# Sliding-window attention into a gated feed-forward block on one core: batch 2's first scores moved into the gate blocks of group 1, and two weight loads cut in half

## The chip, the cores and the metric

The kernel runs on one core of a Trainium2 chip. Its engines are TensorE (PE in the profile; PEld is its loading of weights), VectorE (DVE), ScalarE (ACT), GpSimd (POOL) and SyncE (SP), each with an instruction stream of its own that runs in order. 16 DMA engines, shared by all that issue transfers, move data. The metric is the device time of one execution in microseconds (us); the kernel before takes 339.22 us, the median of three runs (338.67 to 339.76).

## The reference

Two parts follow each other. The first is attention over 8 batches of 8 heads, 576 positions and 64 values a head. Each query sees itself and the 127 keys before it, with a penalty that grows with the distance at a slope of its own for each head:

```python
scores = scale * np.matmul(q, k.transpose(0, 1, 3, 2))
bias = slopes[:, None, None] * (-np.abs(rel).astype(np.float32))[None, :, :]
mask = (rel >= 0) & (rel < window)                      # window = 128
scores = np.where(mask, scores + bias[None], -1000000000.0)
attn = np.exp(scores - np.max(scores, axis=-1, keepdims=True))
attn = attn / (np.sum(attn, axis=-1, keepdims=True) + 1e-09)
out = np.matmul(attn, v)
```

The second takes the 8 x 576 = 4608 rows of 512 values that come out (the heads side by side), and puts them through a gated feed-forward block: `gelu(x @ w_gate) * (x @ w_val) @ w_out`, with 1536 columns between.

## The kernel before, in words

**Feed-forward.** The 4608 tokens are worked through in nine groups of 512. For each group, twelve gate blocks (`gate_val`, L623) of 128 columns each: four matmuls of 512 tokens with `w_gate`, four with `w_val`, each half into a PSUM bank of its own; ScalarE applies gelu to the first (L647) and VectorE multiplies it with the second (L648) into `hT`. Then sixteen out units (`out_part`, L670): three matmuls each of 128 tokens with `w_out` (L677), four units to a tile of 128 tokens in one PSUM bank, which VectorE or ScalarE copies out (L682) and SyncE stores (L667). Group 0 is special: its blocks are worked in pieces of 192, 384 and 128 tokens, as attention of batch 0 hands them over, and its weights come while it runs.

**Attention.** Attention lies between the parts of the groups: batch 1 in group 0, batch 2 and the scores of batch 3 in group 1, and in each later group the products of one batch and the scores of the next. Its steps are: queries and keys loaded by GpSimd (L112) and transposed by a DMA that SyncE issues (`transposes_dma`, L173); `scores` (L235) in two visits `s` of two pairs of heads each, with matmuls of 64x64 tiles (L216), exponentials on ScalarE (L229) and a multiplication by the decay mask on VectorE (L232); `values_and_sums` (L512), the products with v and with ones (L501) in two halves, whose sums are inverted by ScalarE as exp(-ln) (L531, L533) or by a reciprocal on VectorE (L529), and a scaling into the transposed input `xT` of the feed-forward (L537). `scores2` (L267) is a form for the batches from 3 on. ScalarE needs one function table for exponentials and one for gelu, and loads it when the function changes; `exp_table` (L938) loads the first ahead of need.

**Order.** The order in each engine's stream is written out by hand: it is the order of the calls. What lies between a group's gate blocks and the end of its out units is a list in `todo` (L921): a number is that many out units, `("s", b, s, pairs)` scores, `("pv+", b, half)` products, `("scale",)` the scaling that the products left over. PSUM has eight banks, and each tile of `bank()` (L68) takes one until its last reader is done.

**Loads.** GpSimd issues loads one after the other, and each waits until the eighth before it has landed. In places it first copies two values into `mark` (L949, L971, L987), which has it wait for what it copies: at L987, for the last of batch 2's transposed queries, before it issues the loads of batch 3's queries and keys and batch 2's v (L988, L989). At the start it loads batch 0's v, the weights of blocks 0 and 1 by themselves, v's last two blocks of rows, and the weights of blocks 2 and 3 together (L742 to L747).

**Batch 0's rest.** Tokens 384 to 575 of batch 0 are divided by their sums late: `products_rest` (L597) has ScalarE copy the products into `recip` and part of the sums (the last 64 tokens) into `inverse`, a float view of the tile `T`; `inverse_rest` (L609) takes reciprocals of the other 128 tokens straight from PSUM into `inverse`, and `inverse_next` (L613) those of the copied ones, in place; `scale_rest` (L617) multiplies.

**Halves.** `HALVED` (L29) names gate blocks whose matmuls are cut into two of 256 tokens, in both halves of the weights.

Of the kernel before, what the change touches and what calls it, by code (L numbers as in the profile page):

```python
# [26 lines left out]
HANDOVER = 720  # L27

HALVED = ((1, 0), (1, 1))  # L29


@with_exitstack
def kernel(
# [10 lines left out]
    nc = tc.nc  # L44
    B, H, S, D = q.shape
# [22 lines left out]
    def bank():  # L68
        return psum.tile([128, 512], FP32, name="ps")
# [7 lines left out]
    wg = consts.tile([128, 4, DFF], BF16, name="wg")  # L77
# [30 lines left out]
    def load(t, src, b, js=range(5), last=0):  # L108
        for j in js:
            n = rows(j)  # L110
            at = last if j == 4 else 0
            nc.gpsimd.dma_start(  # L112
                out=t[at:at + n, j, :].rearrange("p (h d) -> p h d", h=H),
                in_=src[b][:, 128 * j:128 * j + n, :].rearrange("h p d -> p h d"))
# [5 lines left out]
    def load_v(b, js=range(5)):  # L120
        load(vb[b % 2], v, b, js, 64)
# [20 lines left out]
    def load_w(lo, hi):  # L142
        for dst, src in ((wg, moe_w_gate), (wv, moe_w_val)):
            nc.gpsimd.dma_start(  # L144
                out=dst[:, :, lo:hi],
                in_=src[:, lo:hi].rearrange("(c p) f -> p c f", p=128))
# [44 lines left out]
    def prob(b):  # L191
        return Ps[b % 2].rearrange("p (c i) n -> p c i n", i=2)
# [21 lines left out]
    def score(b, c, i, m, q0, n, out, first=True):  # L214
        half = slice(64 * i, 64 * i + 64)
        nc.tensor.matmul(  # L216
            out=out, lhsT=keys(b, c, m)[half, :], rhs=qT[b % 2][half, c, q0:q0 + n],
            start=first, stop=True, skip_group_check=not first)

    def blocks(n, x):  # L220
        if n == 3 and x:
            return ((7, 448, 128, 0), (8, 512, 64, 128))
        return ((2 * n + x, 128 * n + 64 * x, 192, 0),)
# [11 lines left out]
    def scores(b, s, cs, later=None):  # L235
        pss = []
        for c in cs:
            ps = [bank(), bank()]
            pss.append(ps)
            for n in (2 * s, 2 * s + 1):  # L240
                for x in (0, 1):
                    for m, q0, w, skip in blocks(n, x):
                        for i in (0, 1):
                            col = 192 * (n - 2 * s) + skip
                            score(b, c, i, m, q0, w, ps[i][64 * x:64 * x + 64, col:col + w])
        for c, ps in zip(cs, pss):
            dst = prob(b)[:, c, :, 64 + 384 * s:448 + 384 * s]
            for i in (0, 1):
                exp(dst[:, i, :], ps[i][:, 0:384])
            args = (dst, decay(s, c))  # L250
            if later is None:
                mask(*args)
            else:
                later.append(args)
# [142 lines left out]
    sumrow, recip = {}, {}  # L397
# [188 lines left out]
    def scale_first(c, x, ps):  # L586
# [6 lines left out]
    lo0 = PARTS[0][1][0]  # L593
    inverse = T.rearrange("p h x -> p (h x)").bitcast(FP32)[:, 0:4 * (S - lo0)].rearrange(
        "p (c x) -> p c x", c=4)

    def products_rest():  # L597
        w = S - lo0
        pss = products(0, [(2 * n, slice(2 * n, 2 * n + 2), lo0, S, 0) for n in (0, 1)] + [
            (1 + c // 2 * 2, c, lo0, S, w * (c % 2)) for c in range(4)])  # L600
        for n in (0, 1):
            nc.scalar.copy(out=recip[0][:, 2 * n:2 * n + 2, lo0:S],
                           in_=pss[1 + 2 * n][:, 0:2 * w].rearrange("p (c x) -> p c x", c=2))
        for n in (0, 1):
            nc.scalar.copy(out=inverse[:, 2 * n:2 * n + 2, 128:w],
                           in_=pss[2 * n][:, 0:2 * w].rearrange("p (c x) -> p c x", c=2)[:, :, 128:w])
        return pss

# [2 lines left out]
        nc.vector.reciprocal(inverse[:, c, 0:128], pss[c // 2 * 2][:, at:at + 128])  # L611

    def inverse_next(n):  # L613
        to = inverse[:, 2 * n:2 * n + 2, 128:S - lo0]
        nc.vector.reciprocal(to, to)

    def scale_rest(lo, hi):  # L617
        nc.vector.tensor_tensor(out=xT[:, :, lo:hi], in0=recip[0][:, :, lo:hi],
# [4 lines left out]
    def gate_val(g, f, lo=0, hi=512, later=None):  # L623
        if g not in hid:
            hid[g] = h_pool.tile([128, NF, 512], BF16, name="hT")
        t0 = 512 * g % RING
        n = hi - lo

        if n > 256 or lo >= 384:
            pg, pv = bank()[:, 0:n], bank()[:, 0:n]  # L630
            order = [(w, ps, c, c == 0) for w, ps in ((wg, pg), (wv, pv)) for c in range(4)]
        else:
            ps = bank()
            pg, pv = ps[:, 0:n], ps[:, n:2 * n]
            order = [(w, ps, c, w is wg and c == 0)
                     for cs in ((0, 1), (2, 3)) for w, ps in ((wg, pg), (wv, pv)) for c in cs]
        cols = ((0, 256), (256, 512)) if (g, f) in HALVED else ((0, n),)
        for w, ps, c, begins in order:
            for a, e in cols:
                nc.tensor.matmul(  # L640
                    out=ps[:, a:e], lhsT=w[:, c, 128 * f:128 * (f + 1)], rhs=xT[:, c, t0 + lo + a:t0 + lo + e],
                    start=begins and a == 0, stop=(c == 3),
                    skip_group_check=n <= 256 and lo < 384 or len(cols) > 1)

        def act():
            gl = g_pool.tile([128, 512], BF16, name="gelu")
            nc.scalar.activation(out=gl[:, 0:n], in_=pg, func=AF.Gelu)  # L647
            nc.vector.tensor_tensor(out=hid[g][:, f, lo:hi], in0=pv, in1=gl[:, 0:n],  # L648
                                    op=ALU.mult)

        if later is None:
            act()
        else:
            later.append(act)
# [77 lines left out]
    for h in (0, 2, 4, 6):  # L732
        for w, src in ((0, q), (1, k)):
            (nc.scalar if w and h == 0 else nc.sync).dma_start(
                out=raw[w][h // 4].rearrange("p (h x) -> p h x", h=4)[:, h % 4:h % 4 + 2, :],
# [7 lines left out]
    load_v(0, (0, 1, 2))  # L743
    load_w(0, 128)
    load_w(128, 256)
    load_v(0, (3, 4))
    load_w(256, 512)  # L747

    for h in range(H):
        nc.vector.memset(slope1[:, h:h + 1], -8.0 * 2.0 ** (-8.0 * (h + 1) / H))  # L750
# [6 lines left out]
    for x in (0, 1):  # L757
        half, to = slice(64 * x, 64 * x + 64), slice(64 * x, 64 * x + 192)
# [104 lines left out]
    masks, waiting = [], []  # L863
# [42 lines left out]
    for n in range(4):  # L906
        nc.gpsimd.dma_start(
            out=wo[:, 3 * n:3 * n + 3, :],
# [5 lines left out]
    for t in (qs[0], ks[0]):  # L914
# [5 lines left out]
    scales = []  # L920
    todo = {  # L921
        0: [("table",), ("s", 1, 0, (0, 1)), ("o", 0, 0, 0), ("o", 0, 1, 0), ("s", 1, 0, (2, 3)), ("o", 0, 0, 1), ("s", 1, 1, (0, 1)), ("o", 0, 1, 1), ("s", 1, 1, (2, 3), masks), ("pv+", 1, 0), 4, ("transposes", 2), ("pv+", 1, 1), 4],
        1: [("table",), ("s", 2, 0, (0, 1)), 3, ("s", 2, 0, (2, 3)), 2, ("s", 2, 1, (0, 1)), 2, ("s", 2, 1, (2, 3), masks), ("pv+", 2, 0, scales), 1, ("scale",), 2, ("pv+", 2, 1), 1, 2, ("s2", 3, 0), ("add", 3, 0), 3, ("s2", 3, 2), ("add", 3, 2, None, (0,))],
    }

    def steps(g):
# [11 lines left out]
    def exp_table():  # L938
        nc.scalar.preload_act_table_set("natural_log_exp_and_others")
# [4 lines left out]
    for g in range(NG):  # L944
        if 1 <= g < B - 2:
            transposes_dma(3 if g == 1 else g + 2)
        if g == 1:

            nc.gpsimd.tensor_copy(out=mark, in_=kT[1][0:1, 0, 512:514])  # L949
            load_qk(4)  # L950
            load_v(3)
        for f in range(9 if g == 0 else 0, NF):
            gate_val(g, f)
            if g == 2 and f == 2:
                add(3, 2, act, (1,))
            if g == 0 and f == 10:
                masks_of_last_blocks(0, 8)
            if g == 0 and f == 9:
                for c in range(4):
                    for w in (0, 1):  # L960
                        transpose(1, w, c, (act, dve)[w])
            if 2 <= g < B - 1:
                if f == (4 if g == 2 else 3):
                    sums4(g + 1)
                if f == (6 if g == 2 else 5):
                    gather(g + 1)
                if f == (8 if g == 2 else 7):
                    spread_dma(g + 1)
                if f == 9 and g + 2 < B:

                    nc.gpsimd.tensor_copy(out=mark, in_=hid[g][0:1, f, 0:2])  # L971
                    if g + 3 < B:
                        load_qk(g + 3)
                    load_v(g + 2)
        if g == 0:
            nc.gpsimd.memset(Ps[0][:, :, 0:64], 0.0)
            for t in (qs[1], ks[1]):
                nc.gpsimd.memset(t[64:128, 4, :], 0.0)
        for item in steps(g):
            if isinstance(item, int):  # L980
                out_part(g, item)
            else:
                RUN[item[0]](*item[1:])
        store()
        if g == 0:

            nc.gpsimd.tensor_copy(out=mark, in_=qT[0][0:1, 0, 512:514])  # L987
            load_qk(3)  # L988
            load_v(2)  # L989
# [30 lines left out]
```

## Time and profile before

| what | value |
| --- | --- |
| median of 3 runs | 339.22 us (338.67, 339.76) |
| the profiled execution's own time | 338.56 us |
| its span, first to last instruction | 336.8 us |
| TensorE busy | 331.0 us, 98% of the span |
| VectorE, ScalarE, GpSimd busy | 191.9, 170.7, 108.2 us |
| granted TensorE clock | 1.000 |
| chain that ended last | TensorE 83%, DMA 11%, GpSimd 4% |
| GpSimd's DMA queue | 107456 packets, 18.10 MB |

The profile is of one execution. Busy is the share of time in which an engine has an instruction under way; for TensorE, whose matmuls overlap, 98% says that it seldom stops, not that it runs at its peak. The chain goes back from the last instruction, at each step to what released it. In a timeline a row has start, length, engine, line, instruction, what is written and read and how often, and in brackets the idle time before it and what ended that. In the chain of waits a row has start, length and what; "issue" is time in which the engine waited for nothing that the profile shows. For a load, start is its issue on GpSimd; it has landed when all sixteen DMA engines have reported.

### The profile page before, as it was taken

The numbers are of one execution on the slowest core, as the hardware profiler recorded it, in microseconds if no ns is written. First come the engines' busy times: TensorE is split into PE (matmuls) and PEld (weight loads), VectorE is DVE, ScalarE is ACT, GpSimd is POOL, SyncE is SP. The second block draws the span as 40 slices with busy tenths as digits, with TensorE's granted clock in tenths as the row PEclk, the third lists the DMA queues.
The fourth block names the chain that finished last, engine by engine and source line by source line (L and its number), as shares of the span: only waits on it lengthen the run. The fifth ranks groups of instructions, "written<-read, shape, count | busy, mean of one in ns | idle before, by whom it ended". The sixth has DMA issues, their size and how long they took to land.

```text
span 336.8 us, 8136 instructions
## 1 busy us (share of the span) xinstructions
PE 331.0 (98%) x3316; PEld 169.3 (50%) x3316; DVE 191.9 (57%) x359; ACT 170.7 (51%) x320; POOL 108.2 (32%) x144
## 2 busy tenths in 40 slices
PE   8999999999999999999999999999999999999996
PEld 5657656544554454445544554445444544444444
DVE  7768876435779557945694469536964324303320
ACT  7974687437796339332943375335732133223322
POOL 6974784293094193009500870050000000000000
DMA  8999999999999899969985999495106110020002
GB/s 208 170 198 189 203 166 177 132 167 143 192 148 161 197 168 210 157 144 131 191 168 91 161 179 183 78 173 90 65 2 140 64 65 0 1 95 31 0 31 95
DMA packets 149914, 43.49 MB, mean 129 GB/s; under 512 B 133588, under 2 KB 142836, under 8 KB 149876
## 3 DMA queue, kind: packets, MB, share of 16 engines
q0 software_dynamic: 107456, 18.10, 70.9%
q1 hardware_dynamic: 39104, 18.62, 24.0%
q10 hardware_dynamic: 3316, 6.25, 8.1%
q8 instruction: 26, 0.43, 0.5%
q14 instruction: 12, 0.10, 0.1%
HBM read 43.65 MB, written 9.53 MB: 158 GB/s over the span
## 4 chain that ended last, share of the span: by engine, by line
PE 83%; DMA 11%; POOL 4%; issue 1%; DVE 0%; SPq 0%; ACT 0%; DVEq 0%
PE ps L640 49%; PE ps L677 23%; PE ps L501 4%; DMA vb<-in_v_dram 3%; DMA qT<-qs 2%; PE ps L298 2%; DMA qs<-in_q_dram 2%; DMA wv<-in_moe_w_val_dram 2%; PE ps L697 2%; POOL vb L112 2%; DMA wo<-in_q_dram 1%; PE ps L437 1%; PE ps L713 1%; POOL wg L144 1%; PE ps L154 1%
## 5 line engine op out<-in xcount | busy, mean ns | idle before, releaser
L648 DVE TENSOR_TENSOR hT<-ps,gelu 128x512 bf16<-128x512 f32 (+3 forms) x117 | 73.2, 644 | 92.2 <-PE ps L640 87.3
L647 ACT ACTIVATE gelu<-ps 128x512 bf16<-128x512 f32 (+3 forms) x117 | 65.1, 565 | 100.7 <-PE ps L640 98.8
L640 PE MATMUL ps<-xT,wv 128*128 128x512 bf16 (+4 forms) x476 | 112.8, 359 | 0.5 <-DMA wv<-in_moe_w_val_dram 0.5
L640 PE MATMUL ps<-xT,wg 128*128 128x512 bf16 (+4 forms) x476 | 112.9, 360 | 0.0
L677 PE MATMUL ps<-wo,hT 128*128 128x512 bf16 x396 | 90.3, 380 | 0.0
L640 PEld LDWEIGHTS <-wv 128*128 128x128 bf16 x476 | 45.4, 98 | 49.0 <-DMA wv<-in_moe_w_val_dram 0.9
L640 PEld LDWEIGHTS <-wg 128*128 128x128 bf16 x476 | 44.7, 98 | 47.5 <-DMA wg<-in_moe_w_gate_dram 0.4
L677 PEld LDWEIGHTS <-hT 128*128 128x128 bf16 x396 | 37.0, 98 | 43.4 <-issue 0.2
L229 ACT ACTIVATE P<-ps 128x512 bf16<-128x512 f32 (+1 forms) x108 | 51.4, 579 | 1.9 <-PE ps L216 1.5
L232 DVE TENSOR_TENSOR P<-P,emask 128x768 bf16<-128x768 bf16 x60 | 31.2, 555 | 18.4 <-ACT P L229 16.4
L682 ACT COPY osb<-ps 128x512 f32<-128x512 f32 x27 | 15.9, 588 | 50.8 <-PE ps L677 50.8
L112 POOL DMA_DIRECT2D vb<-in_v_dram x40 | 34.1, 888 | 4.3 <-issue 1.3
L112 POOL DMA_DIRECT2D qs<-in_q_dram x30 | 25.1, 856 | 2.4 <-issue 1.8
L112 POOL DMA_DIRECT2D ks<-in_k_dram x30 | 25.4, 890 | 0.5 <-DMA qs<-in_q_dram 0.3
L971 POOL COPY mark<-hT 1x2 bf16<-1x2 bf16 x4 | 0.7, 174 | 76.3 <-DVE hT L648 76.3
L501 PE MATMUL ps<-P,vb 64*64 64x192 bf16 (+2 forms) x752 | 17.6, 220 | 0.2
L565 DVE TENSOR_TENSOR xT<-ps,rb 128x512 bf16<-128x512 f32 (+3 forms) x34 | 14.7, 502 | 4.6 <-PE ps L501 4.6
L501 PEld LDWEIGHTS <-vb 64*64 64x64 bf16 x752 | 14.8, 107 | 3.5 <-issue 2.4
L385 DVE TENSOR_TENSOR T<-P 64x1024 bf16<-64x1024 bf16 x20 | 13.7, 686 | 0.6
L442 DVE RECIPROCAL r<-ps 128x128 f32<-128x128 f32 (+1 forms) x10 | 9.8, 1021 | 0.0
L298 PEld LDWEIGHTS <-kT 64*64 64x64 bf16 x440 | 7.5, 107 | 4.4 <-issue 4.4
L647 ACT ACT_TABLE_LOAD x7 | 9.0, 1283 | 1.3 <-PE ps L640 1.3
(95 smaller groups left out, 185.0 us busy)
## 6 DMA issues: line engine op xcount, KB each, us to landing
out_dram<-osb SPq DMA_DIRECT2D x35, 256.0 KB
rb<-rd ACTq DMA_DIRECT2D x10, 576.0 KB
vb<-in_v_dram POOLq DMA_DIRECT2D x32, 128.0 KB, 6.7
qs<-in_q_dram POOLq DMA_DIRECT2D x24, 128.0 KB, 5.4
ks<-in_k_dram POOLq DMA_DIRECT2D x24, 128.0 KB, 6.4
wo<-in_moe_w_out_dram POOLq DMA_DIRECT2D x4, 384.0 KB, 12.3
wg<-in_moe_w_gate_dram POOLq DMA_DIRECT2D x5, 256.0 KB, 8.1
wv<-in_moe_w_val_dram POOLq DMA_DIRECT2D x5, 256.0 KB, 8.7
```

The lines of the kernel that those rows point to most:

```text
L112: nc.gpsimd.dma_start(out=t[at:at + n, j, :].rearrange("p (h d) -> p h d", h=H), in_=src[b][:, 128 * j:128 * j + n, :].rearrange("h p d -> ...
L229: nc.scalar.activation(out=dst, in_=src, func=AF.Exp, scale=0.125)
L232: nc.vector.tensor_tensor(out=dst, in0=dst, in1=m, op=ALU.mult)
L298: mm = nc.tensor.matmul(out=ps[64 * x:64 * x + 64, col:col + w], lhsT=keys(b, c, m)[half, :], rhs=qT[b % 2][half, c, q0:q0 + w], start=Tru ...
L385: nc.vector.tensor_tensor(out=to[half, :, x:x + 7:2], in0=P[half, :, 0:10:3], in1=P[half, :, 1:11:3], op=ALU.add)
L501: mm = nc.tensor.matmul(out=out, lhsT=lhsT, rhs=prob(b)[half, c, i, col:col + q1 - q0], start=all(t[2] != u for t in todo[:n]), stop=True, ...
L565: nc.vector.tensor_tensor(out=xT[:, c, at:at + e - a], in0=src, in1=recip[b][:, c, a:e], op=ALU.mult)
L640: nc.tensor.matmul(out=ps[:, a:e], lhsT=w[:, c, 128 * f:128 * (f + 1)], rhs=xT[:, c, t0 + lo + a:t0 + lo + e], start=begins and a == 0, st ...
L647: nc.scalar.activation(out=gl[:, 0:n], in_=pg, func=AF.Gelu)
L648: nc.vector.tensor_tensor(out=hid[g][:, f, lo:hi], in0=pv, in1=gl[:, 0:n], op=ALU.mult)
L677: nc.tensor.matmul(out=acc[g], lhsT=hid[g][:, f, 128 * t:128 * (t + 1)], rhs=wo[:, f, :], start=(f == 0), stop=(f == NF - 1))
L682: (nc.vector.tensor_copy if g < B - 2 and t in by_dve.get(g, (0,)) else nc.scalar.copy)(out=osb, in_=acc[g])
```

## The change

Four edits:

- The first visit of scores of batch 2 for the first two pairs of heads, `("s", 2, 0, (0, 1))`, leaves the list of group 1 and is called in the loop of gate blocks, behind block 6, with a load of the exponential table before it. In the list, one out unit then stands between the last scores and the first products with v, where none stood; before these products there are six out units in all instead of seven, and the last run of units in the list has four instead of three.
- The loads of the weights of blocks 2 and 3 are issued apart: block 2's before batch 0's last two blocks of v, block 3's behind them.
- The copied sums of batch 0's last 64 tokens go into a part of `recip` that is free by then, and the reciprocal is written from there into `inverse`.
- In block 2 of group 1, the gate half alone is cut into matmuls of 256 tokens.

```diff
 HALVED = ((1, 0), (1, 1))
+HALVED_GATE = ((1, 2),)
...
         for n in (0, 1):
-            nc.scalar.copy(out=inverse[:, 2 * n:2 * n + 2, 128:w],
+            nc.scalar.copy(out=recip[0][:, 2 * n:2 * n + 2, 0:w - 128],
                            in_=pss[2 * n][:, 0:2 * w].rearrange("p (c x) -> p c x", c=2)[:, :, 128:w])
...
     def inverse_next(n):
-        to = inverse[:, 2 * n:2 * n + 2, 128:S - lo0]
-        nc.vector.reciprocal(to, to)
+        w = S - lo0
+        nc.vector.reciprocal(inverse[:, 2 * n:2 * n + 2, 128:w], recip[0][:, 2 * n:2 * n + 2, 0:w - 128])
...
-        cols = ((0, 256), (256, 512)) if (g, f) in HALVED else ((0, n),)
         for w, ps, c, begins in order:
+            halves = (g, f) in HALVED or w is wg and (g, f) in HALVED_GATE
+            cols = ((0, 256), (256, 512)) if halves else ((0, n),)
...
     load_w(128, 256)
+    load_w(256, 384)
     load_v(0, (3, 4))
-    load_w(256, 512)
+    load_w(384, 512)
...
-        1: [("table",), ("s", 2, 0, (0, 1)), 3, ("s", 2, 0, (2, 3)), 2, ("s", 2, 1, (0, 1)), 2, ("s", 2, 1, (2, 3), masks), ("pv+", 2, 0, scales), 1, ("scale",), 2, ("pv+", 2, 1), 1, 2, ("s2", 3, 0), ("add", 3, 0), 3, ("s2", 3, 2), ("add", 3, 2, None, (0,))],
+        1: [("table",), ("s", 2, 0, (2, 3)), 3, ("s", 2, 1, (0, 1)), 2, ("s", 2, 1, (2, 3), masks), 1, ("pv+", 2, 0, scales), 1, ("scale",), 2, ("pv+", 2, 1), 1, 2, ("s2", 3, 0), ("add", 3, 0), 4, ("s2", 3, 2), ("add", 3, 2, None, (0,))],
...
             gate_val(g, f)
+            if g == 1 and f == 6:
+                exp_table()
+                scores(2, 0, (0, 1))
```

More of the change, by code (lines that the diff above doesn't have):

```diff
@@ L642, in gate_val @@
                     start=begins and a == 0, stop=(c == 3),
-                    skip_group_check=n <= 256 and lo < 384 or len(cols) > 1)
+                    skip_group_check=n <= 256 and lo < 384 or halves)
         def act():
```

## The prediction

> **What bounds the kernel now.** I read the chain of waits first, then TensorE's instructions in time around each place that the change touches, then GpSimd's and SyncE's, and last the landings of the loads one by one.
>
> The page's busy line and the chain, in order of time:
>
> ```profile
> PE 331.0 (98%) x3316; PEld 169.3 (50%) x3316; DVE 191.9 (57%) x359; ACT 170.7 (51%) x320; POOL 108.2 (32%) x144
> ...
> 13.61 6.82 DMA wv<-in_moe_w_val_dram
> ...
> 56.55 8.35 DMA qT<-qs
> 64.90 0.05 issue
> 64.95 0.18 POOL mark L987
> ...
> 66.07 7.03 DMA qs<-in_q_dram
> ...
> 75.11 10.93 DMA vb<-in_v_dram
> 86.03 0.04 issue
> 86.08 1.00 PE ps L501 x26
> 87.08 2.05 PE ps L677 x9
> ```
>
> TensorE is the bound nearly everywhere, but up to 86.08 us the chain is one of transfers: queries of batch 2 transposed, GpSimd's mark that waits for them, the loads of batch 3's queries and keys, then batch 2's v. After 97 us the chain holds TensorE alone. So what the change does to the time is settled by 97 us, at the few places where TensorE waits. These are two, in TensorE's timeline:
>
> ```profile
> 18.40 0.81 PE L640 MATMUL ps<-xT,wv 128*128 128x384 bf16 x4
> 19.18 0.82 PE L640 MATMUL ps<-xT,wg 128*128 128x384 bf16 x4
> 20.48 0.82 PE L640 MATMUL ps<-xT,wv 128*128 128x384 bf16 x4 [0.47 <-DMA wv<-in_moe_w_val_dram]
> ...
> 85.34 1.07 PE L501 MATMUL ps<-P,vb 64*64 64x192 bf16 x14
> 85.73 0.10 PEld L501 LDWEIGHTS <-vb 64*64 64x64 bf16 x1 [0.32 <-issue]
> 86.07 0.21 PEld L501 LDWEIGHTS <-vb 64*64 64x64 bf16 x12 [0.24 <-DMA vb<-in_v_dram]
> ```
>
> Four such matmuls take 0.65 us where nothing waits. From 18.40 to 19.18 is 0.13 more, from 19.18 to 20.48 is 0.65 more: block 2 of group 0 waits 0.78 us for its weights. In batch 2's first products, two gaps: to 85.73 (0.29 over, released by the first exponential of the last scores, which frees a PSUM bank) and to 86.08 (0.26 over, released by the second 128-row block of v, which landed at 86.03). Without waits TensorE could be 1.3 us ahead here; that is all there is to gain.
>
> **The change part by part.**
>
> *The moved products and the out unit.* Before the first products of batch 2, seven out units run now and six will. A unit is 3 matmuls; 9 take 1.94 us from first start to last end in steady pace (0.216 each), so a unit is 0.65. It goes behind the products (3 units become 4). The scores only move; they issue no DMA, and on ScalarE and VectorE their four exponentials and two masks pass ahead of the gelus and products of blocks 7 to 11. But the last scores now have an out unit between themselves and the products, and each passage between 128x128 and 64x64 tiles costs TensorE 0.10 (a 512-column matmul starts 0.31 before such a tile instead of 0.21): two more passages, 0.19. The bank wait of 0.29 goes, since the unit gives the exponentials 0.65 + 0.19.
>
> *The new wait at gate block 6.* The moved scores need batch 2's transposed keys. SyncE issues that transpose here:
>
> ```profile
> 56.55 2.28 SPq L182 DMA_TRANSPOSE qT<-qs  x1
> 63.35 3.06 SPq L175 DMA_TRANSPOSE kT<-ks  x1
> 66.52 1.04 SPq L667 DMA_DIRECT2D out_dram<-osb  x2
> ```
>
> In the record of its semaphore the sixteen completions come from 68.71 to 70.30 us. Block 6 ends at 69.82 now and will end 0.3 to 0.8 earlier, so TensorE waits there about 1 us, with blocks 7 to 11 behind it. Then: scores 0.46, block 7 at 70.8; from block 7 to the products is 85.12 - 69.82 = 15.30 now, less the scores at their old place (0.55 with passages), less 0.65, plus 0.19: 14.3. The products start at 85.05 and want the second block of v 0.3 later, 85.4. It comes at 86.03. TensorE waits 0.6 more. So both waits end before, or with, one event: the landing of v.
>
> *What sets that landing.* No step of TensorE, ScalarE or VectorE stands in its chain: GpSimd issues loads, each after the eighth before it has landed; the DMA engines are busy throughout to 62 us; the first query block of batch 2 lands at 49.91 and SyncE, waiting, issues its transpose at 49.97; the mark waits for the last one (64.90). A TensorE that is early gains nothing there. The landing moves only with the loads.
>
> *Weights of blocks 2 and 3 apart.* GpSimd's rows:
>
> ```profile
> 11.28 1.63 POOL L112 DMA_DIRECT2D vb<-in_v_dram  x2
> 12.87 0.80 POOL L144 DMA_DIRECT2D wg<-in_moe_w_gate_dram  x1
> 13.61 0.79 POOL L144 DMA_DIRECT2D wv<-in_moe_w_val_dram  x1
> ```
>
> Two issues more, 1.5 us of GpSimd, hidden because five to eight loads are under way. The halves for block 2 go out at 11.28 and 12.03 and land, at 0.74 each behind 16.49, by 18.0; block 2 wants them at 19.05 and 19.70, so its wait of 0.78 goes. Batch 0's v blocks 3 and 4 land near 19.3 instead of 17.77, wanted at 20.4: hidden by 1.1. The halves of block 3 land by 20.8, wanted at 21.7. Part of the 0.78 is taken back at once: four products banks are wanted at 20.45, when blocks 0 to 2 still hold six of eight and X (first gelu done 20.4, its product 20.9). Nothing of it reaches the end, as the wait for v swallows it.
> What does reach the end is the DMA time. Four half loads replace two whole ones. By landings, whole ones come 1.33 apart (20.43 to 28.45, six), half ones 0.74 (13.58 to 15.79 for fifteen of sixteen engines): 2.96 for 2.66, +0.3. By packet times (60 ns for 512 B, 41 ns for 256 B; 512 packets each on 16 engines, scaled by 1.33/1.93 as whole loads overlap) it is 3.65, +1.0. Below, it could be nothing, if a gap further on takes it up. I take +0.4, near the landings, since these are what is waited for. The DMA engines have no gap until 62 us, so it is carried to every later landing, keys and v of batch 2 alike.
> The Trainium skill's "DMA: Bandwidth & Descriptors", Specifications, puts the least size for line rate at 512 B and says that smaller ones become read-modify-writes, which speaks against this part. Were a 256 B packet as dear as a 512 B one, four loads would cost 5.3 and the delay would be 2.7; the 41 ns row says otherwise.
>
> *Table loads.* Two more on ScalarE (1.28 each): before the moved exponentials and before gelu 7. Four exponentials take 1.64. From scores at 70.3: exponentials done 72.4, table 73.7, gelu 7 at 74.3, VectorE's product 75.0 (the two masks, 0.56 each, lie before it). Block 7's banks are wanted by block 11 at 77.7: hidden by 2.7. If that cover went, up to 2.6 would show.
>
> *Halved gate of block 2, group 1.* 8 matmuls of 256 for 4 of 512: halved blocks start 1.77 and 1.75 apart, whole ones 1.73; half a block is +0.01 to 0.02, before the wait for v. *The separate reciprocal:* VectorE idles 1.2 us before its first reciprocal for ScalarE's two copies; they no longer hold it, and the scaling that block 8 needs (done 28.4, wanted 28.99) comes up to 1.2 earlier. It only keeps an early TensorE from waiting there.
>
> *After the products.* The out copy of the second tile falls behind the scaling on VectorE (0.69); the next products use their last two banks 0.47 and 0.58 into their run and the scaling frees its second bank at about 89.65. I allow 0.05 (bounds 0 and 0.6, if they were given the bank of that late copy).
>
> *Sum.* The products end with v's landing, at 87.0 + 0.4. Behind it one unit more, 0.65, and 0.05: +1.1. The profiled execution took 338.56 us (span 336.8), 0.66 under the median of 339.22, so I add 1.1 to both: 339.7 for it, 340.3 for the median.
>
> **The rivals.** A measurement here can tell about 0.3% (1.02 us) from no change: the three times span 338.67 to 339.76.
>
> *Lighter.* Queries' last transpose had fifteen engines done at 63.39 and one at 64.90, after a fetch of instructions held that engine (a 16 KB packet from 62.04, 1.75 us). TensorE's instructions come at other times after the change; if the fetch misses this, v lands up to 1.5 earlier, and the wait for keys bounds instead, 0.6 below: 0.65 + 0.4 - 0.6 = +0.4, 339.7. For it: the engine is one of sixteen. Against: other landings show such laggards too (14.63 after 13.58).
>
> *Heavier.* Half loads at their packet times, +1.0, or the bank of the late copy, +0.6: +1.7 to 1.9, about 341.0. For it: landings near 14 us were 0.9 apart with a laggard.
>
> *Faster.* If v landed before TensorE wants it: the 0.78 and 0.55 go, two passages come: -1.1, 338.1. It decides when v's second block lands before 84.2 and keys before 69.1, 1.8 and 1.2 sooner. Against: nothing in the change speeds a load, and one that is earlier by the laggard's 1.5 is not enough.
>
> The Trainium skill's "TensorE: Matmul & The Clock Gate", Part 1, says one idle window of about 3.4 us halves the clock. The granted clock is 1.000 throughout with waits up to 0.65; no row shows a wait of 1 us after warm-up. If the wait at block 6 tripped it, some 1.7 us would be added; by the page it shouldn't.
>
> **How the numbers follow.** Forecast 0.50 (339.9 to 340.7), lighter 0.20 (339.2 to 339.9), heavier 0.20 (340.7 to 342), faster 0.10. Slower by over 0.3% (above 340.24): the heavier case and three fifths of the forecast, 0.5. Within: the lighter and two fifths of the forecast, 0.4. Faster: 0.1. The range, 338.7 to 341.6, leaves out most of the faster case and the end of the heavier one.
>
> **What would show it.** Right: no wait in block 2 of group 0; a wait of about 1 us for keys at the moved scores and 0.4 to 0.8 for v in batch 2's first products; v's second block landing near 86.4; one unit more between that and group 2; nothing but TensorE after 97 us. Wrong: products that start without waiting for v, or a landing of v outside 85 to 87.5, or waits for banks in gate blocks 8 to 11.

## The result, and the profile after

The changed kernel takes 341.36 us (median of 8 executions, 339.06 to 343.50) against 338.74 for the kernel before in the same set (8 executions, 338.35 to 339.76): a ratio of 1.0068, with a 95% interval from 1.0044 to 1.0092. It is slower, and its times lie further apart: 4.4 us from end to end instead of 1.4. The same kernel was measured twice more beside the experiments, on two chips, with 1.0012 [0.9995, 1.0029] and 1.0051 [1.0027, 1.0076]. All three together say that it costs between nothing that can be told and 0.9%. The spread is a part of the result that has to be explained. Below, an execution over 1.5% above the fastest of its kernel (344.60, 346.57 and 343.81) counts as slow, and no reading rests on it.

The profiled execution took 341.34 us (span 339.6). First the busy line and the chain of waits (start, length, what), as shown of before:

```profile
PE 332.4 (98%) x3320; PEld 170.4 (50%) x3320; DVE 192.8 (57%) x359; ACT 173.3 (51%) x322; POOL 109.7 (32%) x146
...
34.10 13.05 DMA wo<-in_moe_w_out_dram
47.20 0.81 PE ps L699 x3
...
54.30 2.00 PE ps L502 x74
56.44 1.24 SPq L183
...
57.86 7.32 DMA qT<-qs
65.17 0.05 issue
65.23 0.17 POOL mark L993
...
68.06 7.67 DMA qs<-in_q_dram
75.73 0.28 issue
76.01 12.04 DMA vb<-in_v_dram
88.05 0.04 issue
88.09 1.00 PE ps L502 x26
89.09 2.05 PE ps L679 x9
```

From the queries' transpose on the chain is the same as before, and ends again at batch 2's v: the second block of v landed at 88.05 instead of 86.03. Ahead of it another load stands in the chain, the last one of `w_out`, for which TensorE waited 0.61 us up to 47.20; the same load landed at 45.25 before, and nothing waited for it. The two rows between, TensorE's products of batch 1 and SyncE's issue of the transpose behind them, stand in the chain of before too, 1.1 and 1.2 us earlier:

```profile
53.21 2.00 PE ps L501 x74
55.21 1.16 SPq L182
```

TensorE's timeline at the three places that the prediction named:

```profile
18.58 0.81 PE L642 MATMUL ps<-xT,wg 128*128 128x384 bf16 x4
19.23 0.81 PE L642 MATMUL ps<-xT,wv 128*128 128x384 bf16 x4
19.88 0.81 PE L642 MATMUL ps<-xT,wg 128*128 128x384 bf16 x4
...
70.06 1.03 PE L642 MATMUL ps<-xT,wv 128*128 128x512 bf16 x4
72.51 0.52 PE L217 MATMUL ps<-qT,kT 64*64 64x192 bf16 x16 [1.42 <-DMA kT<-ks]
72.96 1.04 PE L642 MATMUL ps<-xT,wg 128*128 128x512 bf16 x4
...
87.53 0.29 PE L502 MATMUL ps<-P,vb 64*64 64x192 bf16 x4
88.09 0.34 PE L502 MATMUL ps<-P,vb 64*64 64x64 bf16 x10 [0.27 <-DMA vb<-in_v_dram]
...
99.72 1.04 PE L642 MATMUL ps<-xT,wg 128*128 128x512 bf16 x4
```

Block 2 of group 0 (the three rows from 18.58) now follows in steps of 0.65, without its old wait. Instead TensorE stands 1.42 us before the moved scores, for batch 2's keys, and 0.27 in the products, for v. The last row is the first matmul of group 2, at 99.72; it was at 96.94 before, 2.78 earlier, and the two executions differ by 2.78 us in all. What is between v's landing and group 2 grew from 10.91 (96.94 - 86.03) to 11.67 (99.72 - 88.05), by 0.76: the out unit that now stands behind the products. The remaining 2.02 is v's later landing (88.05 - 86.03). The loads were about as late before the mark already: batch 2's first queries landed at 51.86 instead of 49.91, 1.95 later. Whether the change made them late isn't shown.

### The profile page after: what moved, and what is told of

Its sections match the earlier page's. It is cut to its first block, busy times and chain, and to the rows that moved or that the text cites. A ratio compares the mean times of both kernels' runs of the same rounds, so it can differ in the third digit from the quotient of the medians.

```text
span 339.6 us, 8150 instructions
## 1 busy us (share of the span) xinstructions
PE 332.4 (98%) x3320; PEld 170.4 (50%) x3320; DVE 192.8 (57%) x359; ACT 173.3 (51%) x322; POOL 109.7 (32%) x146
## 4 chain that ended last, share of the span: by engine, by line
PE 83%; DMA 12%; DVE 1%; issue 1%; POOL 1%; ACT 1%; SPq 0%; DVEq 0%
PE ps L642 47%; PE ps L679 23%; PE ps L502 5%; DMA wo<-in_moe_w_out_dram 4%; DMA vb<-in_v_dram 4%; DMA qs<-in_q_dram 2%; PE ps L299 2%; DMA qT<-qs 2%; PE ps L75 1%; PE ps L438 1%; PE ps L217 1%; PE ps L715 1%; POOL qs L113 1%; PE ps L699 1%; PE ps L795 0%
## 5 line engine op out<-in xcount | busy, mean ns | idle before, releaser
L233 DVE TENSOR_TENSOR P<-P,emask 128x768 bf16<-128x768 bf16 x60 | 31.2, 556 | 21.1 <-ACT P L230 19.0
```

What stands on the lines that cost most here:

```text
L233: nc.vector.tensor_tensor(out=dst, in0=dst, in1=m, op=ALU.mult)
```

## The experiments

**The theories.** *V*: the time is set by the landing of batch 2's v, and the out unit behind it is the loss; with a unit more before the products the loss goes. *Keys*: the scores behind block 6 want the keys at about the time at which they land, and lose whatever the keys are late; with the scores at their old place the loss goes. *Weights*: the half loads of blocks 2 and 3 delay every later landing; alone, or taken back, they show it. *Clock*: the new waits are long enough to lower TensorE's granted clock.

All ratios are to the kernel before in the same set of runs, with 95% intervals; each set ran on one chip, and the three chips differ. Unless said otherwise there were 12 executions of each kernel, and 35, 35 and 32 of the kernel before.

### First set: one part at a time

The seventh unit back in front of the products, all else as changed:

```diff
-... ("s", 2, 1, (2, 3), masks), 1, ("pv+", 2, 0, scales), ... ("add", 3, 0), 4, ...
+... ("s", 2, 1, (2, 3), masks), 2, ("pv+", 2, 0, scales), ... ("add", 3, 0), 3, ...
```

> The changed kernel with one out unit taken from the last run of group 1 (four to three) and put before the first products of batch 2 (two instead of one behind the last scores, seven in all as before the change). Landing theory: the products of batch 2 end with the landing of v's second block (88.05 us in the changed kernel's profile), whatever stands before them, so a unit that moves ahead of that is free: 0.65 less than the changed kernel, 340.7 beside its 341.4, with a wait for v of 0 to 0.1. Keys theory (the loss is the wait for keys behind gate block 6, 1.6 us there, and v's landing only ends it by accident): the unit fills at most the 0.43 of v's wait, 340.9 or more. Theory that the waits don't matter: no difference.

Measured: 339.18 us (338.29 to 344.60), ratio 1.0012 [0.9997, 1.0027]. Most of the loss is gone by that number, but the changed kernel itself had the same ratio in the second set, so the unit's share can't be read from this run alone. Nor does its profile (340.42) help: keys (68.90) and v (86.11) landed before they were wanted there, and the time went to a halved clock from 16.13 to 19.55, long before the changed parts of group 1.

The scores back in the list, with the unit still behind the products:

```diff
-1: [("table",), ("s", 2, 0, (2, 3)), 3, ("s", 2, 1, (0, 1)), 2, ("s", 2, 1, (2, 3), masks), 1, ("pv+", ...
+1: [("table",), ("s", 2, 0, (0, 1)), 2, ("s", 2, 0, (2, 3)), 2, ("s", 2, 1, (0, 1)), 1, ("s", 2, 1, (2, 3), masks), 1, ("pv+", ...
...
-            if g == 1 and f == 6:
-                exp_table()
-                scores(2, 0, (0, 1))
```

> The changed kernel with the moved scores back at the head of group 1's list, six out units before the products as in the changed kernel (2, 2, 1, 1). Landing theory: the wait for keys (1.6 us) goes from gate block 6, and the wait for v grows by the same, from 0.43 to about 2; the time stays that of the changed kernel, 341.4 within 0.5. Keys theory: 1.6 less, 339.8, and v's wait stays at 0.4.

Measured: 339.83 us (338.42 to 342.40), ratio 1.0031 [1.0009, 1.0052]. So a loss remains without any wait for keys. The profiled execution, the slowest of the twelve, shows more than the wait for v. TensorE's timeline, then its windows (stretch, length, busy time and count of PE, PEld, DVE, ACT and POOL, granted clock, DMA share, GB/s):

```profile
85.53 0.46 PE L502 MATMUL ps<-P,ones 64*64 64x384 bf16 x8
87.28 0.90 PE L502 MATMUL ps<-P,vb 64*64 64x192 bf16 x14 [1.29 <-DMA vb<-in_v_dram]
```

```profile
84.30:87.70 3.40, 1.78 (x26) 0.70 (x25) 1.07 (x3) 2.00 (x6) 0.00 (x0) 1.00 2.08 153
87.70:91.10 3.40, 3.40 (x41) 1.93 (x42) 1.63 (x3) 2.12 (x4) 0.00 (x0) 0.51 1.69 213
91.10:94.50 3.40, 3.40 (x110) 2.31 (x109) 1.83 (x4) 0.70 (x2) 0.29 (x2) 0.99 0.60 194
```

TensorE works for 1.78 of 3.4 us, and for the 3.4 after that its clock is 0.51: matmuls take twice as long. The wait for v is 1.29 us, for a landing at 87.65. In this execution 13.13 us pass from that landing to group 2 (100.78), 11.67 and 1.46 more.

The weights of blocks 2 and 3 apart, in the kernel before, and nothing else:

```diff
     load_w(128, 256)
+    load_w(256, 384)
     load_v(0, (3, 4))
-    load_w(256, 512)
+    load_w(384, 512)
```

> The kernel before with the weight loads of blocks 2 and 3 apart, and nothing else. Landing theory: TensorE comes up to 0.78 earlier, as block 2's wait goes, but v lands 0.4 to 0.8 later for the two loads more (28.45 to 29.47 us for the last of these weights in the two profiles), so the time rises by about that much: 339.2 to 339.5 beside 338.74 for the kernel before; the wait at batch 2's first products grows from 0.55 to some 1.7. Rival, that the wait for weights is what counts: 0.5 to 0.8 less, 338.0.

Measured: 338.85 us (337.62 to 339.62), ratio 0.9996 [0.9983, 1.0010]. The delay is there in this pair of profiles: counted from the landing of GpSimd's first load, the last of the weights that go out ahead of batch 1's queries landed after 19.60 us here (28.77 - 9.17) and after 19.18 before (28.45 - 9.27), 0.42 later (0.4 was predicted). It is no more than one pair: over the twelve profiles with half loads the same count runs from 18.76 to 20.42, and the other one with whole loads, weights_whole, has 18.48. And v landed at 84.98 in this execution, the fastest of its twelve, 1.05 earlier than in that of before. No loss is seen at the end.

The scores back in the list, and the first two blocks of v issued ahead of the mark, so that nothing waits for v:

```diff
+            load_v(2, (0, 1))
             nc.gpsimd.tensor_copy(out=mark, in_=qT[0][0:1, 0, 512:514])
             load_qk(3)
-            load_v(2)
+            load_v(2, (2, 3, 4))
```

> As the kernel with the scores back in the list, and the first two blocks of batch 2's v are loaded ahead of the mark, before batch 3's queries and keys, so that they land near 66 us; the other three blocks where they were. Landing theory: the wait for v goes (2 us), and TensorE has no wait left up to batch 3's scores: about 1.1 less than the kernel before, 337.7, if batch 3's keys (landed 91.9 before, wanted at 93.0) don't come late; if they do, up to 1 more. Keys theory: as the kernel with the scores back, less at most 0.4.

Measured: 338.70 us (338.42 to 340.75), ratio 1.0004 [0.9989, 1.0019]. v landed at 65.41, and nothing waited for it. Against scores_back, 339.83 in the same set, that is 1.1 us, and all of the loss. Yet the kernel before isn't beaten, where 1.1 us less was expected. One piece of that is a wait for a PSUM bank, which scores_back had too (VectorE's copy of an out tile, `osb`, gives the bank). The row shows 0.21 us of it; by the starts, from the scores' first matmul at 83.01 to the next out unit at 83.94, where the visit before took 0.46, it cost 0.47:

```profile
83.65 0.36 PE L217 MATMUL ps<-qT,kT 64*64 64x192 bf16 x9 [0.21 <-DVE osb L684]
```

### Second set: the place of the scores, and v early

The changed kernel again, and with `f == 6` made `f == 9`; then both of these with the first two blocks of v ahead of the mark.

> The changed kernel itself, beside the variants of this call. The kernel with the scores back in the list, which differs in the place of the scores alone, took 339.8, and its profile shows a half-clock window of 3.4 us behind its wait for v. Landing theory: the two end at the same landing, so 339.8 within 0.5 here too, and what the first eight runs have beyond (341.4) is v landing later in that set. Keys theory: the wait at block 6 is a loss of its own, so 341 to 341.5 again.

Measured: 339.37 us (338.33 to 340.90), ratio 1.0012 [0.9995, 1.0029]. In this set the changed kernel can't be told from the kernel before. Its profiled execution had keys at 70.66, where they cost 0.29 by the starts of the matmuls, and v at 85.53, before it was wanted. Group 2 began at 97.59, 26.93 after the keys.

> The changed kernel with the moved scores behind gate block 9 instead of 6, some 5 us later, when the keys have landed in every profile so far (68.9 to 72.5). The wait for keys goes; the wait for v grows by as much, to 1.5 to 2 in one piece. Landing theory: the time of the changed kernel in this call, within 0.4. Keys theory: 1.0 to 1.6 less. A clock theory beside them: one wait of over 1.5 us halves the clock for a window of 3.4 us (1.7 us lost), which two shorter waits do less often, so some executions are 1.7 longer and the spread stays at 3 to 4 us.

Measured: 339.67 us (338.86 to 340.97), ratio 1.0017 [1.0001, 1.0032]. The keys landed late, at 72.18, and nothing waited for them; what they no longer cost came back as a longer wait for v:

```profile
84.75 0.46 PE L502 MATMUL ps<-P,ones 64*64 64x384 bf16 x8
85.84 0.28 PE L502 MATMUL ps<-P,vb 64*64 64x192 bf16 x4 [0.63 <-DMA vb<-in_v_dram]
86.46 0.34 PE L502 MATMUL ps<-P,vb 64*64 64x64 bf16 x9 [0.34 <-DMA vb<-in_v_dram]
```

From v (86.42) to group 2 (98.09) it is 11.67 us again, what the changed kernel had.

> The changed kernel with the first two blocks of batch 2's v loaded ahead of the mark. The wait for v goes, the wait for keys behind block 6 stays at 1 to 1.6 and now sets the end. Landing theory: earlier by the part of v's wait that the keys leave, 0.4 to 0.6, and by no more: 0.5 less than the changed kernel of this call. Keys theory says the same of v, and 1 to 1.5 more for the next kernel.

Measured: 340.14 us (338.14 to 346.57), ratio 1.0038 [1.0009, 1.0066]. Without 346.57 and 343.81 the highest is 342.60 and the median 339.58. Its profiled execution was a good one (338.26 us, keys at 67.47, v at 65.23), so that it doesn't show what the long ones wait for. The one of 342.60 had a granted clock of 0.995 over the whole execution. A loss in the clock is thus in it; that the keys came late to block 6 there is argued, not seen.

> Both: the moved scores behind block 9 and the first two blocks of v ahead of the mark. No wait is left but batch 3's scores for PSUM (0.2). By either theory about 0.8 less than the kernel before (0.4 of block 2's weights, 0.55 of the first products, less 0.19 for two passages between tile sizes): 338.0 beside 338.85, spread under 2 us as no wait over 0.4 is left. Wrong if batch 3's keys come late, then a wait at 92 to 93 us.

Measured: 339.15 us (338.55 to 341.42), ratio 1.0010 [0.9989, 1.0030]. No wait for keys or v. The highest is 341.42, and 342.60 in v_early, with the scores three blocks later as the only difference; one execution each doesn't say much. No gain over the kernel before either, where 0.8 us less was expected: waits for banks take the place of those for transfers. By the starts these two cost 0.28 and 0.56 us, more than their brackets show:

```profile
79.66 2.10 PE L679 MATMUL ps<-wo,hT 128*128 128x512 bf16 x9 [0.21 <-ACT gelu L649]
85.83 0.41 PE L502 MATMUL ps<-P,vb 64*64 64x192 bf16 x12 [0.42 <-DVE osb L684]
```

### Third set: the changed kernel's spread, and a better one

> The changed kernel a third time, beside three variants. Medians so far are 341.36 (8 executions) and 339.37 (12), the kernel before 338.74 and 338.86. If the difference between the sets is where v lands (88.05 and 85.53 us in their profiles), a third set lies between or at one of them, 339.2 to 341.4, and the first-products wait of its profile explains its time: start of group 2 is 11.67 us behind v's landing whenever TensorE waited for it.

Measured: 340.80 us (339.14 to 342.53; 9 executions), ratio 1.0051 [1.0027, 1.0076]. The profiled execution took 342.29. TensorE's timeline, then its windows:

```profile
68.57 1.03 PE L642 MATMUL ps<-xT,wv 128*128 128x512 bf16 x4
72.11 0.53 PE L217 MATMUL ps<-qT,kT 64*64 64x192 bf16 x16 [2.51 <-DMA kT<-ks]
72.56 1.04 PE L642 MATMUL ps<-xT,wg 128*128 128x512 bf16 x3
73.44 1.81 PE L642 MATMUL ps<-xT,wv 128*128 128x512 bf16 x4
75.04 1.91 PE L642 MATMUL ps<-xT,wg 128*128 128x512 bf16 x4
```

```profile
70.00:73.50 3.50, 1.34 (x20) 0.78 (x22) 0.48 (x2) 1.66 (x4) 2.48 (x4) 1.00 1.78 227
73.50:76.90 3.40, 3.40 (x10) 1.24 (x9) 1.72 (x3) 2.53 (x4) 2.56 (x3) 0.50 2.12 150
76.90:80.00 3.10, 3.10 (x16) 1.37 (x15) 0.98 (x2) 1.19 (x2) 1.64 (x3) 0.99 1.89 151
```

Here the keys are the whole loss: TensorE is ready at 69.6 and stands still until they land at 72.06; then from 73.53 to 76.94 its clock is halved, which costs half of 3.41 us, 1.7. The products find v (86.41) long there. Group 2 comes 28.62 after the keys, where after_again, without a halved clock, had 26.93: the difference is 1.69.

> The changed kernel with seven out units before the first products, as in the earlier run of it, now in the same call as the changed kernel. Landing theory: where v is waited for, group 2 starts 0.65 sooner behind v's landing (11.0 in place of 11.67); executions in which it isn't waited for stay. So 0.3 to 0.65 less than the changed kernel of this call. The rival, that out units only change places, says no difference.

Measured: 339.58 us (338.18 to 341.29), ratio 1.0017 [1.0000, 1.0033]; by medians 1.2 us less than the changed kernel in the same set, more than a unit's 0.65. Over all their executions (24 and 29, on several chips) the medians are 339.39 and 339.82, 0.4 apart. That fits a seventh unit that takes back a part of the loss, while the keys keep the rest, but it isn't shown: the two ratios' intervals overlap. The profiled execution (340.85) lost its time to the keys, and group 2 came 26.76 after them:

```profile
72.51 0.52 PE L217 MATMUL ps<-qT,kT 64*64 64x192 bf16 x16 [1.78 <-DMA kT<-ks]
```

> The changed kernel with the weights of blocks 2 and 3 loaded together again. If the two loads more are what sends v later, 0.3 to 0.4 less than the changed kernel of this call (the last of those weights landed 0.4 earlier behind the first load in the kernel before than with the split alone). If the loads' jitter behind the mark is larger than that, no difference, though TensorE loses the 0.4 that the earlier weights gave it, as that lies ahead of the wait for v.

The changed kernel with `load_w(256, 512)` in one again. Measured: 339.26 us (338.63 to 341.32), ratio 1.0016 [1.0000, 1.0032]. By medians that is 1.5 us less than the changed kernel in the same set, yet its profiled execution (341.32) has the same fault, keys at 72.28:

```profile
72.33 0.52 PE L217 MATMUL ps<-qT,kT 64*64 64x192 bf16 x16 [2.31 <-DMA kT<-ks]
```

So keys come late without the half loads too. Whether the half loads make it more frequent stays open: the two ratios' intervals overlap (from 1.0027 and to 1.0032), and the same changed kernel had 1.0012 in another set.

Last, the scores and the order of units as before, no halved gate, the weights apart and the separate reciprocal kept, and the first two blocks of v ahead of the mark:

> The list of the kernel before, with the weights apart, the reciprocal of the changed kernel, and the first two blocks of batch 2's v ahead of the mark; no moved scores, no halved gate. TensorE gains 0.4 at block 2, v is no longer waited for (0.26), the bank wait at the products stays (0.29): 0.65 less than the kernel before, 338.2. If loads ahead of the mark hold back the keys (as in the kernel with v early and scores behind block 6, whose executions ran from 338.1 to 346.6), nothing here wants these keys before 78 us, so the spread should stay under 2 us.

Measured: 338.22 us (337.84 to 339.07), ratio 0.9981 [0.9970, 0.9993], by that 0.6 us faster than the kernel before, with a spread of 1.2 us, the narrowest of the experiments. The kernel before with early v alone wasn't run, so what the weights and the reciprocal add to it is not told apart. Its keys landed at 72.05, as late as in after_third, and cost nothing. The products run without a wait for v:

```profile
84.92 0.53 PE L217 MATMUL ps<-qT,kT 64*64 64x192 bf16 x20
85.27 0.45 PE L502 MATMUL ps<-P,ones 64*64 64x384 bf16 x8
85.50 0.79 PE L502 MATMUL ps<-P,vb 64*64 64x192 bf16 x14
```

### What the runs say together

An execution's time less the start of group 2's first matmul is 241.6 us in twelve of the fourteen profiles (241.61 to 241.65), and 242.1 in two (v_early and weights_whole, where TensorE stood some 0.2 and 0.3 us at 127 and 130). So the time is the start of group 2 plus that, and for the changed kernel this start is the latest of two events:

| profiled execution | us | keys landed | wait for keys | v landed | wait for v | group 2 begins | set by |
| --- | --- | --- | --- | --- | --- | --- | --- |
| before | 338.56 | 70.30 | 0 | 86.03 | 0.52, with the bank's | 96.94 | v + 10.91 |
| changed, result | 341.34 | 72.46 | 1.42 | 88.05 | 0.38 | 99.72 | v + 11.67 |
| changed, second set | 339.21 | 70.66 | 0.29 | 85.53 | 0 | 97.59 | keys + 26.93 |
| changed, third set | 342.29 | 72.06 | 2.51 | 86.41 | 0 | 100.68 | keys + 26.93 + 1.69 of clock |
| weights whole | 341.32 | 72.28 | 2.31 | 86.41 | 0 | 99.22 | keys + 26.94 |
| block 9 | 339.74 | 72.18 | 0 | 86.42 | 1.28 | 98.09 | v + 11.67 |

Wait for keys is the bracket in the timeline (by the starts in the second set). Wait for v is what batch 2's first products took beyond the 1.36 us of back_v_early (84.69 to 86.05), where nothing waits. Keys landed between 67.5 and 72.5 in the fourteen profiled executions of all kernels, v (where it wasn't loaded early) between 85.0 and 88.1. In the kernel before the scores stand behind block 11 and want the keys at 78.5: six us of cover even for the latest. Behind block 6 they want them at 69.3 to 71.0 (72.1 in units7, after its halved clock), in the middle of that spread.

## Why the prediction was right or wrong

The direction was right, and the median of 341.36 lies 1.0 us above the predicted 340.3, near the range's upper end. Part of that nearness is luck: the prediction started from 339.22, and the kernel before took 338.74 in the result's set, so that by medians 2.6 us were lost where 1.1 was predicted. The two other sets gave, by their ratios, +0.4 and +1.7 us. Two of its own signs of being wrong came true: v landed at 88.05 in the result's profile, outside the 85 to 87.5 that it named, and in the two other profiles of the changed kernel the products did not wait for v.

- *Two waits in the place of those removed; the time set by a landing.* Right in the result's profile; in the other two it was one wait and the landing of the keys. The weight wait of 0.78 in block 2, and the bank wait of 0.29, are gone, and none of it reached the end, in all executions of the changed kernel that were profiled.
- *One out unit behind v's landing, 0.65 + 0.05.* Right: 0.76, and 11.67 in two kernels.
- *Nothing but TensorE after 97 us.* Right: 241.6 in twelve profiles, 0.5 more in two.
- *No step of TensorE, ScalarE or VectorE stands in v's chain.* Wrong for TensorE: in both chains its products of batch 1 stand right before SyncE's issue of the queries' transpose (53.21 before, 54.30 in the result's profile). Since the loads were late as well, how much of v's 2.0 us came by way of TensorE isn't shown. At the mark only 0.3 of it is to be seen (queries' last transpose done at 65.17 against 64.90), because one of the sixteen engines had held that transpose back by 1.5 us in the profile of before. From the mark's start to v's landing it is 22.8 us instead of 21.1.
- *A wait of about 1 us at block 6, with the keys 0.6 below v.* This is the step that failed. Its one landing, 70.30, came from one execution, and so did the distance from keys to v, 15.73 us. Over the profiles the wait was 0.29, 1.42 and 2.51, and the distance, where v is loaded behind the mark, 14.13 to 17.21. With keys at 72 and 14.3 to v, it is the keys that set the end. In two of three profiles of the changed kernel they did.
- *+0.4 of DMA time from the half loads.* 0.42 at the weights in one pair of profiles, within a scatter larger than that. As a step towards the end it isn't borne out: split_alone has no loss (0.9996, at most 0.3 us by its interval), and some 50 us later the scatter of v's landing, 85.0 to 88.1, is seven times as large.
- *The clock wouldn't fall.* Wrong in some executions. The Trainium skill's "TensorE: Matmul & The Clock Gate", Part 1, speaks of a whole idle window of about 3.4 us, and by that a wait of 1 to 2.5 us is safe. The runs differ. The halved stretches begin on multiples of 3.413 us after the clock's first rise, as the traces record both (after_third: rise at 5.26, and 20 x 3.413 later 73.53; scores_back: 5.82, and 24 x 3.413 later 87.74; units7: 5.89, and 3 x 3.413 later 16.13). In the stretch before its fall TensorE had stood for 1.99 us in after_third (the part of the 2.51 that lies after 70.12), and for 1.59 in scores_back (busy for 1.82 of the 3.41), 1.29 of it in one piece. units7_again had 1.78 within one stretch (busy for 1.63) and kept its clock. So did the result's profile and weights whole, where an edge at 71.90 and one at 71.21 cut the 1.42 and the 2.31 in two (busy for 2.2 to 2.8 of each 3.41). Of the changed kernel's 29 executions, three had a mean clock of 0.994 or 0.995 (343.50, 342.53 and 342.29, the slowest of their sets); of 102 of the kernel before, in the three sets of experiments, one (340.35, at 0.995). The price, 1.7, was right (1.69 in after_third).
- *The "lighter" rival, by the laggard of the queries' transpose.* Its condition came true (65.17 for all of qT in the result's profile, with no engine 1.5 us behind), and v was later all the same. The laggard doesn't set v's landing alone.
- *Hidden parts.* The table loads, the halved gate block (0.88 against 0.865 between starts) and the separate reciprocal cost nothing that shows, as predicted. From the products to group 2 it is 0.76 more than before (10.69 from 89.02, and 9.93 from 87.01), 0.11 beyond the unit, where 0.05 was allowed for the late out copy.

Why the keys land up to 5 us apart from one execution to the next stays open in part. Their transpose is issued between 61.5 and 65.1, right behind the landing of their last load. It takes 6.0 to 7.0 us in the five profiles in which that is 1.4 us or more ahead of the mark, and 7.3 to 8.4 in the nine in which it is less than 1 ahead; of these the result's profile is one (64.86 and 65.23, 7.6 us), while before had 63.35 and 64.95, and 6.95 us. So it takes longer where it runs beside the loads that the mark releases; no run changed that alone, and it stays an observation. Open too is why the changed kernel has so many long executions in the result's set.

## What to carry to other kernels

A landing read from one profile is a sample. Before work is moved up to a transfer, compare the slack that it leaves with the scatter of that landing over several executions: here a planned wait of 1 us stood against 5 us of scatter, and in the profiles the late half of that scatter was what cost time. Where the end of a stage waits for a load, bring the load forward and leave the consumer: two blocks of v issued ahead of a barrier gave 0.6 us, together with the weights apart and the separate reciprocal, where the change that moves the work that consumes keys and v lost 0.4 to 2.3. When a wait goes, look at what holds the next resource; without the waits for transfers, waits for PSUM banks cost 0.47 us in one kernel and 0.84 in another.

## What the runs showed of the hardware that was not expected

- Waits of TensorE well below 3.4 us can halve its clock. Two stretches of 3.41 us in which it was busy for 1.37 and 1.82 us were followed by one at 0.50 or 0.51; another with 1.63 was not, so that busy time alone doesn't decide. A third case lies at the start: in units7 it was busy for 2.31 of the 3.41 us up to 16.13, and had 0.50 from there to 19.55, so that a thin mixture of small instructions seems to do it too; scores_back, busy for 2.41 of the 3.41 up to 16.06, kept its clock. Where the threshold lies isn't settled.
- Landings of one program scatter by several microseconds from execution to execution (keys 67.5 to 72.5), while everything from group 2 on repeats to 0.04 us in twelve of the fourteen profiles.
